# Decode attention with a gated MLP on one core: the output products move between the halves of the next head's score products, and an output weight moves from the fourth row to the fifth

## The chip, the core and the metric

The kernel runs on one core of a Trainium2 chip. The metric is device time in microseconds of one execution, the median of several runs. A core has five engines with instruction streams of their own: TensorE (PE; PEld is its loading of weights), VectorE (DVE), ScalarE (ACT), GpSimd (POOL) and SyncE (SP), which here only issues transfers. They wait for one another through semaphores. Sixteen DMA engines carry the transfers from HBM into SBUF, the on-chip memory of 128 partitions.

## The reference

One token attends to a cache of 8192 positions in 32 heads of 192, and a gated MLP follows:

```python
def _A_ref(x, k_cache, v_cache, wq, wo):          # x: layer norm of the token, 640 wide
    q = (x @ wq).reshape(B, Sq, H, Dh)            # H = 32, Dh = 192
    scores = einsum("bhqd,bhkd->bhqk", q, k_cache) * (Dh ** -0.5)   # Sk = 8192
    p = softmax(scores)
    o = einsum("bhqk,bhkd->bhqd", p, v_cache)
    return o.reshape(B, Sq, H * Dh) @ wo
h = x + _A_ref(layernorm(x), ...)
h2 = h + _B_ref(layernorm(h), W_gate, W_up, W_down)   # (gate * (gate > 0) * up) @ W_down, F = 1536
```

All data are float32. Nearly all bytes are the keys and values: 6.3 MB each for every head.

## The kernel before

The host packs keys, values and weights into long rows, so that each transfer is one block of 128 partitions with up to 16320 columns of 4 bytes, 8160 KB. SBUF has room for three such rows, the slots X, Y and Z. Thirty heads go in ten turns of three units; a prologue row (`row_p`, in Y) has the first head's query weights and keys, and a tail has the last head and the MLP.

The heads of a turn are called a, b, c. In a unit TensorE makes the scores of its head (`pe_k`, two halves of 12 products into `sc`) and the product of the values with the exponentials of the head before it (`pe_v`, 32 products into `po`). The rows of a turn:

- row 1, into X: keys of a, query weights of b, values 0 to 7 of the head before a
- row 2, into Z: that head's values 8 to 31, its output weights (`woa`), first half of b's keys
- row 3, into Y: second half of b's keys, query weights of c, values 0 to 23 of a
- row 4, into X: values 24 to 31 of a, its output weights (`wob`), keys of c
- row 5, into Y: query weights of the next a, all values of b, its output weights (`woc`)

A unit on TensorE, `pe_unit` (L220) and `pe_unit2` (L343) for the third, runs: scores, both halves; values 0 to 23; the next query (`pe_q`, `pe_t`), which waits for VectorE; values 24 to 31; then a wait for ScalarE's copy `ob` of the value products, the output products `pe_o` (into `od`, six small products), a wait for the exponentials, and `pe_l`, their sum (into `pl`). Only then do the next unit's scores begin.

VectorE (`dve_unit`, L404) follows: it transposes both score halves (L400), finds the maximum `mp` (L408), multiplies the next query weights by the token (`dve_d1`, five instructions, L392 and L394), takes the maximum `m` (L411), which the exponentials need, copies `od` to `oc`, adds the output weights times `oc` to `accs` (two instructions, L414 and L415), and makes the factor `mrl` from the sum (L416, L417).

SP (`turn`, L554) issues the five rows in order on one queue. Ahead of each issue it waits until the slot was released and the row before in that slot has landed: row 3 for `free[5]`, row 4 for `free[1]`, row 5 for `free[2]` and `free[3]`, the next rows 1 and 2 together for `free[4]`. VectorE gives `free[4]` behind its second transpose in the third unit (`relay`), `free[2]` at the same place in the second, and `free[5]` at the end of the turn; TensorE gives `free[1]` and `free[3]`, in two steps each, with certain value products and ahead of `pe_q`.

Of the kernel before, what the change touches and what calls it, by code (L numbers as in the profile page):

```python
# [27 lines left out]
W_4 = 8 * PW + OW + KW  # L28
W_5 = QW + KW + OW
# [8 lines left out]
def pack(inputs):  # L38
# [26 lines left out]
    for i in range(NTURN):  # L65
        a, b, c = 3 * i + 1, 3 * i + 2, 3 * i + 3
        va, vb, vv = vc[a - 1], vc[b - 1], vc[c - 1]
        rows[0][i] = cat(kw[a], qw(b), va[:, :8 * PW])
        rows[1][i] = cat(va[:, 8 * PW:], ow(a - 1), kw[b][:, :12 * 512])
        rows[2][i] = cat(kw[b][:, 12 * 512:], qw(c), vb[:, :24 * PW])  # L70
        rows[3][i] = cat(vb[:, 24 * PW:], ow(b - 1), kw[c])
        rows[4][i] = cat(qw(c + 1), vv, ow(c - 1))
# [13 lines left out]
def build(nc, arrays):  # L86
# [46 lines left out]
    def wait(eng, s, n, sub=0, **kw):  # L133
        w = eng.wait_ge(s, n)  # L134
        if sub:
            w.then_inc(s, -sub)
        return w
# [8 lines left out]
    slots = {"p": Y, 1: X, 2: Z, 3: Y, 4: X, 5: Y}  # L146
    k_at = lambda t, off: (lambda half, i: t[:, off + (i + 12 * half) * 512:off + (i + 12 * half + 1) * 512])
    pr_at = lambda t, off, i: t[:, off + i * PW:off + (i + 1) * PW]
# [13 lines left out]
    wob = cut(X, 8 * PW, OW)  # L162
    kc = lambda half, i: cut(X, 8 * PW + OW + (12 * half + i) * 512, 512)
    wqa = cut(Y, 0, QW)
    vcc = lambda i: cut(Y, QW + i * PW, PW)
    woc = cut(Y, QW + KW, OW)
# [14 lines left out]
    def pe_k(blk, before=(None, None)):  # L181
        for half in range(2):
            if before[half] is not None:
                wait(te, before[half], 16)
            for part in range(3):
                for g in range(4):
                    m = te.matmul(sc[Q(g), half * 512:half * 512 + 512], qs[:, 32 * part:32 * part + 32],  # L187
                                  blk(half, part * 4 + g), start=(part == 0), stop=(part == 2))
            op(m, inc=p2d)
# [27 lines left out]
    def pe_l():  # L217
        op(te.matmul(pl[:, 0:1], ones, vec["rs"], start=True, stop=True), inc=p2d)

    def pe_unit(kblk, kwait, vblk, vwait, freed, q_next=True, split=24, inc_at=None):  # L220
        pe_k(kblk, kwait)
        pe_v(vblk, 0, 8, inc_at=inc_at)
        if vwait[0] is not None:
            wait(te, vwait[0], 16)
        pe_v(vblk, 8, 24, inc_at=inc_at)
        if q_next:
            wait(te, d2p, 2, 2)
            if freed is not None:
# [5 lines left out]
        if vwait[1] is not None:  # L234
            wait(te, vwait[1], 16)
        pe_v(vblk, 24, 32, last=p2a)
        n = 2 if q_next else 1
        wait(te, a2p, n, n)
        pe_o()
        wait(te, a2p, 1, 1)  # L240
        pe_l()

    def pe_warm(n):
        for _ in range(n):
            for g in range(4):
                te.matmul(pl[Q(g), :], ones[:, 0:32], ident.rearrange("p c -> p c")[:, None, :].to_broadcast([P, 4, P]),
                          start=True, stop=True)

    def tensor_program():
        wait(te, cst_pe, 1, 1)  # L250
        wait(te, land[0], 16)
# [7 lines left out]
        pe_k(kp)  # L259
# [3 lines left out]
        wait(te, a2p, 2, 2)  # L263
        pe_l()
        with te.Fori(0, NTURN):
            wait(te, land[1], 16)
            pe_unit(ka, (None, None), va, (land[2], None), free[1], inc_at=(7, free[1]))
            pe_unit(kb, (None, land[3]), vb, (None, land[4]), free[3], inc_at=(23, free[3]))
            pe_unit2()
        wait(te, tl["t1"], 16, 16)  # L270
        pe_k(kt)
        pe_v(vt, 0, 8, inc_at=(7, fin))
        wait(te, tl["t2a"], 16, 16)
        pe_v(vt, 8, 24)
        wait(te, d2p, 1, 1)
        pe_t()
        pe_v(vt, 24, 32, last=p2a)
# [65 lines left out]
    def pe_unit2():  # L343
        pe_k(kc)
        wait(te, land[5], 16)
        pe_v(vcc, 0, 24)
        wait(te, d2p, 2, 2)
        pe_q()
        pe_t()
        pe_v(vcc, 24, 32, last=p2a)  # L350
        wait(te, a2p, 2, 2)
        pe_o()
        wait(te, a2p, 1, 1)
        pe_l()

# [25 lines left out]
    def settle(extra=0):  # L381
# [15 lines left out]
    def dve_scores():  # L397
        for half in range(2):
            s = slice(half * 512, half * 512 + 512)
            dv(ve.transpose(st[:, s], sc[:, s]), w=pd())  # L400

    scores = st.rearrange("p (r u) -> p r u", u=16)[:, :, 0]

    def dve_unit(wo_t, w_next, relay=None, q_wait=None):  # L404
        dve_scores()
        if relay is not None:
            wait(ve, ds, cnt.n).then_inc(relay, 1)
        dv(ve.reduce_max(vec["mp"], scores, axis=AX.X), w="self", inc=d2p)  # L408
        if w_next is not None:
            dve_d1(w_next, first=q_wait)  # L410
        dv(ve.reduce_max(vec["m1"], pt[:, 0:P], axis=AX.X, negate=True), w=pd(), inc=d2a)  # L411
        if wo_t is not None:
            dv(ve.tensor_copy(oc, od[:, 0:2]), w=pd())  # L413
            dv(STT(accs[:, 0:D], wo_t[:, 0:D], oc[:, 0:1], accs[:, 0:D], op0=ALU.mult, op1=ALU.add), w="self")  # L414
            dv(STT(accs[:, D:OW], wo_t[:, D:OW], oc[:, 1:2], accs[:, D:OW], op0=ALU.mult, op1=ALU.add))  # L415
        dv(ve.reciprocal(vec["rl"], pl[:, 0:1]), w=pd())  # L416
        dv(ve.tensor_scalar(mrl, id32[:, 0:2], vec["rl"], None, op0=ALU.mult), w="self")  # L417

# [8 lines left out]
    def vector_program():  # L427
        dv(ve.memset(po[:, 0:PW], 0.0))
        dv(ve.memset(accs, 0.0))
        dv(ve.reduce_sum(id32, ident.rearrange("p (g c) -> p c g", c=32), axis=AX.X), w=(cst_ve, 1))  # L430
        wait(ve, cst_ve, 1, 1)
        wait(ve, land[0], 16)
# [10 lines left out]
        dve_scores()  # L443
        dv(ve.reduce_max(vec["mp"], scores, axis=AX.X), w="self", inc=d2p)
        dve_d1(wq1)
        dv(ve.reduce_max(vec["m1"], pt[:, 0:P], axis=AX.X, negate=True), w=pd(), inc=d2a)
        ve.sem_inc(free[5], 1)
        dv(ve.reciprocal(vec["rl"], pl[:, 0:1]), w=pd())
        dv(ve.tensor_scalar(mrl, id32[:, 0:2], vec["rl"], None, op0=ALU.mult), w="self")
        settle()  # L450
        with ve.Fori(0, NTURN):
            dve_unit(woa, wqb)
            dve_unit(wob, wqc, relay=free[2])
            wait_row5 = (land[5], 16)
            dve_unit(woc, wqa, relay=free[4], q_wait=wait_row5)
            settle()
            ve.sem_inc(free[5], 1)
        dve_scores()
        dv(ve.reduce_max(vec["mp"], scores, axis=AX.X), w="self", inc=d2p)
        dv(ve.reduce_max(vec["m1"], pt[:, 0:P], axis=AX.X, negate=True), w=pd(), inc=d2a)  # L460
        dv(ve.tensor_copy(oc, od[:, 0:2]), w=pd())
        dv(STT(accs[:, 0:D], wot[:, 0:D], oc[:, 0:1], accs[:, 0:D], op0=ALU.mult, op1=ALU.add), w="self", inc=d2p)
        dv(STT(accs[:, D:OW], wot[:, D:OW], oc[:, 1:2], accs[:, D:OW], op0=ALU.mult, op1=ALU.add), inc=d2p)
        dv(ve.reciprocal(vec["rl"], pl[:, 0:1]), w=pd())
        dv(ve.tensor_scalar(mrl, id32[:, 0:2], vec["rl"], None, op0=ALU.mult), w="self")
# [34 lines left out]
    def scalar_program():  # L500
# [3 lines left out]
        act_qs()  # L504
        act_exp()
# [40 lines left out]
    def sync_program():  # L546
        load(Y[:, 0:W_P], dram["row_p"], land[0])
# [3 lines left out]
        wait(sp, free[5], 1, 1)  # L551
        wait(sp, land[0], 16, 16)

        def turn(i):  # L554
            load(Y[:, 0:W_3], r3[i], land[3])
            wait(sp, free[1], 2, 2)
            wait(sp, land[1], 16, 16)
            load(X[:, 0:W_4], r4[i], land[4])
            wait(sp, free[2], 1, 1)
            wait(sp, land[2], 16, 16)  # L560
            wait(sp, free[3], 2, 2)
            wait(sp, land[3], 16, 16)
            load(Y[:, 0:W_5], r5[i], land[5])
            wait(sp, free[4], 1, 1)
            wait(sp, land[4], 16, 16)

        with sp.Fori(0, NTURN - 1) as i:
            turn(i)
            load(X[:, 0:W_1], r1[i + 1], land[1])
            load(Z[:, 0:W_2], r2[i + 1], land[2])  # L570
            wait(sp, free[5], 1, 1)
            wait(sp, land[5], 16, 16)
# [35 lines left out]
```

## Time and profile before

| | |
|---|---|
| median of 3 runs | 1045.81 us (1042.98 to 1047.77) |
| the profiled execution, its own time | 1047.05 us |
| its span, first to last instruction | 1045.8 us |
| TensorE busy | 562.2 us, 54% |
| VectorE busy | 189.7 us, 18% |
| ScalarE busy | 40.8 us, 4% |
| mean granted TensorE clock | 0.742 |
| moved by DMA | 446.07 MB, mean 427 GB/s |

The span covers the profiled execution only, and times inside it count from its first instruction. In rows of the timeline the first number is the start, the second the length, both in us; behind the operands stands how many instructions are merged, and in brackets how long the engine was idle before and what ended it. A matmul of float32 shows up as two records, so a unit's 24 score products are x48. In rows of windows stand the bounds, the length, the busy time of PE, PEld, DVE, ACT and POOL, the granted TensorE clock as a share of full speed, the DMA engines' share and GB/s.

### The profile page before, as it was taken

To read this page: it belongs to the slowest core of one execution; us is meant where nothing else is said; L and a number is where in the kernel's file an instruction comes from. 1 tells how busy PE (TensorE), PEld (TensorE's weight loads), DVE (VectorE), ACT (ScalarE), POOL (GpSimd) and SP (SyncE) were. 2 spreads that over 40 slices of the span, in tenths; PEclk is the share of its full clock that TensorE was granted. 3 is DMA by queue.
4 is the path that set the end of the run, shared out by engine and by line. 5 is a ranking of instruction groups with operands and counts; after the bars stand their busy time and mean duration, and the time that the engine had idled before them with its cause. 6 is when DMAs were issued, how large, how long until landed. Compare 5 with 4: busy or idle time off the path is not lost. (4 is left out here: it accounts for less than half of the span.)

```text
span 1045.8 us, 10227 instructions
## 1 busy us (share of the span) xinstructions
PE 562.2 (54%) x4480; PEld 181.9 (17%) x4480; DVE 189.7 (18%) x474; ACT 40.8 (4%) x136; POOL 1.2 (0%) x11
## 2 busy tenths in 40 slices
PE   0645646555373464565644736645465456464566
PEld 0212112111121111121111201211121121121123
DVE  1311212111122122121121211211122112121111
ACT  1000000000000000000000000000000000000000
POOL 0000000000000000000000000000000000000000
PEclk9886767667777677686687776677867767676788
DMA  9999999999999999999999999999999999999998
GB/s 399 438 438 424 419 439 439 436 412 429 434 408 432 439 440 432 437 429 416 439 432 432 413 437 414 433 434 439 424 413 439 437 421 436 422 437 431 414 424 344
DMA packets 8800, 446.07 MB, mean 427 GB/s; under 512 B 980, under 2 KB 1112, under 8 KB 1240
## 3 DMA queue, kind: packets, MB, share of 16 engines
q1 hardware_dynamic: 8788, 445.94, 99.1%
q8 instruction: 7, 0.11, 0.0%
q14 instruction: 1, 0.01, 0.0%
q10 hardware_dynamic: 4, 0.00, 0.0%
HBM read 445.94 MB, written 0.00 MB: 426 GB/s over the span
## 5 line engine op out<-in xcount | busy, mean ns | idle before, releaser
L187 PE MATMUL sc<-slot_x,qs 128*32 128x512 f32 x1008 | 152.3, 767 | 95.1 <-DMA slot_x<-row 85.0
L194 PE MATMUL po<-slot_y,p 128*2 128x384 f32 x1152 | 122.3, 579 | 46.5 <-DMA slot_y<-row 43.7
L194 PE MATMUL po<-slot_z,p 128*2 128x384 f32 x560 | 69.9, 650 | 107.9 <-DMA slot_z<-row 103.3
L400 DVE STREAM_TRANSPOSE st<-sc 128x512 f32<-128x512 f32 x64 | 45.9, 717 | 338.3 <-PE sc L187 338.3
L187 PE MATMUL sc<-slot_y,qs 128*32 128x512 f32 x288 | 55.7, 937 | 75.6 <-DMA slot_y<-row 75.1
L194 PE MATMUL po<-slot_x,p 128*2 128x384 f32 x336 | 43.5, 652 | 94.6 <-DMA slot_x<-row 94.6
L187 PEld LDWEIGHTS sc<-slot_x,qs 128*32 128x32 f32 x1008 | 36.0, 136 | 193.3 <-issue 107.4
L194 PEld LDWEIGHTS po<-slot_y,p 128*2 128x2 f32 x1152 | 30.5, 96 | 138.0 <-issue 84.0
L411 DVE TENSOR_REDUCE m<-pt 128x1 f32<-128x128 f32 x30 | 8.8, 292 | 209.6 <-PE pt L206 209.6
L194 PEld LDWEIGHTS po<-slot_z,p 128*2 128x2 f32 x560 | 14.7, 100 | 153.1 <-DMA slot_z<-row 110.5
L413 DVE COPY oc<-od 128x2 f32<-128x2 f32 x30 | 4.8, 160 | 197.8 <-PE od L213 197.8
L486 ACT COPY qs<-q_ps 128x96 f32<-128x96 f32 x32 | 7.7, 239 | 765.3 <-ACTq L134 765.3
L394 DVE SCALAR_TENSOR_TENSOR prod<-slot_y,xn,prod 128x192 f32<-128x192 f32 x88 | 36.9, 419 | 3.1
L210 PE MATMUL od<-mrl,ob 128*128 128x1 f32 x128 | 22.1, 277 | 24.7 <-PEq L134 24.7
L187 PEld LDWEIGHTS sc<-slot_y,qs 128*32 128x32 f32 x288 | 11.6, 157 | 114.9 <-DMA slot_y<-row 84.2
L210 PEld LDWEIGHTS od<-mrl,ob 128*128 128x128 f32 x128 | 20.3, 227 | 53.1 <-issue 53.1
L194 PEld LDWEIGHTS po<-slot_x,p 128*2 128x2 f32 x336 | 8.3, 94 | 118.4 <-DMA slot_x<-row 96.5
L187 PE MATMUL sc<-slot_z,qs 128*32 128x512 f32 x240 | 27.8, 596 | 0.0
L490 ACT COPY ob<-po 128x384 f32<-128x384 f32 x32 | 15.3, 479 | 192.1 <-ACTq L134 192.1
L201 PE MATMUL q_ps<-pat,prod 128*128 128x96 f32 x64 | 15.5, 326 | 8.5 <-PEq L134 8.5
L394 DVE SCALAR_TENSOR_TENSOR prod<-slot_x,xn,prod 128x192 f32<-128x192 f32 x40 | 16.8, 419 | 1.4
L201 PEld LDWEIGHTS q_ps<-pat,prod 128*128 128x128 f32 x64 | 10.1, 199 | 31.0 <-issue 31.0
(106 smaller groups left out, 249.6 us busy)
## 6 DMA issues: line engine op xcount, KB each, us to landing
slot_x<-row SPq DMA_DIRECT2D x20, 8160.0 KB, 36.8
slot_z<-row SPq DMA_DIRECT2D x10, 8160.0 KB, 42.5
slot_y<-row SPq DMA_DIRECT2D x10, 8160.0 KB, 45.5
slot_y<-row SPq DMA_DIRECT2D x10, 7104.0 KB, 26.9
slot_x<-row_t SPq DMA_DIRECT2D x1, 7680.0 KB, 22.8
slot_y<-row_p SPq DMA_DIRECT2D x1, 7136.0 KB, 19.6
slot_z<-row_t2a SPq DMA_DIRECT2D x1, 5088.0 KB, 34.5
slot_y<-row_up SPq DMA_DIRECT2D x1, 3840.0 KB, 44.4
```

The lines of the kernel that those rows point to most:

```text
L187: m = te.matmul(sc[Q(g), half * 512:half * 512 + 512], qs[:, 32 * part:32 * part + 32], blk(half, part * 4 + g), start=(part == 0), stop=( ...
L194: m = te.matmul(po[32 * g:32 * g + 2, 0:PW], p[:, 2 * i:2 * i + 2], blk(i), start=(i < 4), stop=(i >= 28))
L201: te.matmul(q_ps[:, 0:96], prod[:, 0:P], pat[:, 0, :], start=True, stop=False)
L210: te.matmul(od[:, 0:1], ob[:, k * DH:k * DH + P], mrl[:, k:k + 1], start=(k == 0), stop=(k == 1))
L394: dv(STT(prod, w3[:, j, :], xn[:, j:j + 1], prod, op0=ALU.mult, op1=ALU.add), w="self", inc=d2p if j == DJ - 1 else None)
L400: dv(ve.transpose(st[:, s], sc[:, s]), w=pd())
L411: dv(ve.reduce_max(vec["m1"], pt[:, 0:P], axis=AX.X, negate=True), w=pd(), inc=d2a)
L413: dv(ve.tensor_copy(oc, od[:, 0:2]), w=pd())
L486: op(ac.copy(qs, q_ps[:, 0:96]), inc=a2p)
L490: op(ac.copy(ob, po[:, 0:PW]), inc=a2p)
```

## The change

Three things are changed together.

TensorE: `pe_o` and `pe_l` of a unit move into the next unit, between the two halves of its scores. The scores' first half waits only for the query. `pe_unit2` goes, the third unit uses `pe_unit`, and the waits for rows are given as a table of places.

VectorE: `dve_unit` now begins with the copy `oc` and the factor `mrl` of the head before, then come the transposes, `mp`, the next query, the output weights and `m`. `free[4]` is given once the second score half is done, ahead of the second transpose; `free[2]` and `free[5]` are given behind the output weights, `free[5]` hence in the first unit of the next turn.

Rows: `wob` moves from row 4 (now 15360 columns) to row 5 (now 15168). SP waits for `free[2]` ahead of the next row 1 and no longer ahead of row 5. The prologue's row counts on row 5's semaphore, and the first unit adds a product with zeros (`mrl` is set to zero, `ob` is copied from zeros).

```diff
-W_4 = 8 * PW + OW + KW
-W_5 = QW + KW + OW
+W_4 = 8 * PW + KW
+W_5 = 2 * OW + QW + KW
...
+    def pe_unit(kblk, vblk, rows, freed=None, freed_at=None, q_next=True):
+        def landed(n):
+            if n in rows:
+                s, sub = rows[n]
+                wait(te, s, 16, sub)
+
+        wait(te, a2p, 1, 1)
+        landed("k0")
+        pe_k(kblk, 0)
+        wait(te, a2p, 1, 1)
+        pe_o()
+        wait(te, a2p, 1, 1)
+        pe_l()
+        landed("k1")
+        pe_k(kblk, 1)
+        landed("v0")
...
+    def dve_unit(w_out, w_next=None, freed_k=None, freed_wo=None, row=None):
+        k0 = pd()
+        dve_out()
+        dve_mrl()
+        dve_t(0, w=k0)
+        k1 = pd()
+        if freed_k is not None:
+            wait(ve, *k1).then_inc(freed_k, 1)
+            dve_t(1)
+        else:
+            dve_t(1, w=k1)
+        dve_mp()
+        if row is not None:
+            wait(ve, row, 16)
+        if w_next is not None:
+            dve_d1(w_next)
+        dve_wo(w_out)
+        if freed_wo is not None:
+            wait(ve, ds, cnt.n).then_inc(freed_wo, 1)
+        dve_m1()
...
         with ve.Fori(0, NTURN):
-            dve_unit(woa, wqb)
-            dve_unit(wob, wqc, relay=free[2])
-            wait_row5 = (land[5], 16)
-            dve_unit(woc, wqa, relay=free[4], q_wait=wait_row5)
+            dve_unit(woc, wqb, freed_wo=free[5])
+            dve_unit(woa, wqc, freed_wo=free[2])
+            dve_unit(wob, wqa, freed_k=free[4], row=land[5])
             settle()
-            ve.sem_inc(free[5], 1)
...
         def turn(i):
+            wait(sp, free[5], 1, 1)
+            wait(sp, land[5], 16, 16)
             load(Y[:, 0:W_3], r3[i], land[3])
             wait(sp, free[1], 2, 2)
             wait(sp, land[1], 16, 16)
             load(X[:, 0:W_4], r4[i], land[4])
-            wait(sp, free[2], 1, 1)
-            wait(sp, land[2], 16, 16)
             wait(sp, free[3], 2, 2)
             wait(sp, land[3], 16, 16)
             load(Y[:, 0:W_5], r5[i], land[5])
+            wait(sp, free[2], 1, 1)
+            wait(sp, land[2], 16, 16)
             wait(sp, free[4], 1, 1)
             wait(sp, land[4], 16, 16)
```

The order on TensorE from the end of the second unit into the third, before (`po` are value products, `od` output products, `pl` the sum, `sc` scores; the new kernel's line numbers differ):

```order
L194 MATMUL po<-slot_x,p 2x384 x8
L210 MATMUL od<-mrl,ob 128x1 x2
L213 MATMUL od<-mrl,ob 64x1 x4
L218 MATMUL pl<-rs,ones 128x1
L187 MATMUL sc<-slot_x,qs 32x512 x24
L194 MATMUL po<-slot_y,p 2x384 x24
```

and now, at the same place:

```order
L187 MATMUL po<-slot_x,p 2x384 x8
L180 MATMUL sc<-slot_x,qs 32x512 x12
L203 MATMUL od<-mrl,ob 128x1 x2
L206 MATMUL od<-mrl,ob 64x1 x4
L211 MATMUL pl<-rs,ones 128x1
L180 MATMUL sc<-slot_x,qs 32x512 x12
L187 MATMUL po<-slot_y,p 2x384 x24
```

The output products and the sum have moved behind the first twelve score products.

VectorE in the first unit of a turn, before (`accs` rows are those with the output weights):

```order
L400 STREAM_TRANSPOSE st<-sc 128x512 x2
L408 TENSOR_REDUCE mp<-st 128x1
L392 TENSOR_SCALAR prod<-slot_x,xn 128x192
L394 SCALAR_TENSOR_TENSOR prod<-slot_x,xn,prod 128x192 x4
L411 TENSOR_REDUCE m<-pt 128x1
L413 COPY oc<-od 128x2
L414 SCALAR_TENSOR_TENSOR accs<-slot_z,oc,accs 128x640
L415 SCALAR_TENSOR_TENSOR accs<-slot_z,oc,accs 128x320
L416 RECIPROCAL rl<-pl 128x1
L417 TENSOR_SCALAR mrl<-id,rl 128x2
```

and now:

```order
L373 COPY oc<-od 128x2
L380 RECIPROCAL rl<-pl 128x1
L381 TENSOR_SCALAR mrl<-id,rl 128x2
L385 STREAM_TRANSPOSE st<-sc 128x512 x2
L388 TENSOR_REDUCE mp<-st 128x1
L365 TENSOR_SCALAR prod<-slot_x,xn 128x192
L367 SCALAR_TENSOR_TENSOR prod<-slot_x,xn,prod 128x192 x4
L376 SCALAR_TENSOR_TENSOR accs<-slot_y,oc,accs 128x640
L377 SCALAR_TENSOR_TENSOR accs<-slot_y,oc,accs 128x320
L391 TENSOR_REDUCE m<-pt 128x1
```

The output weights read here are those of row 5 of the turn before (slot Y); with them Y is released, for row 3.

SP in the loop, before (ISA rows are waits alone):

```order
L544 DMA slot_y<-row 128x16320
L544 DMA slot_x<-row 128x16320 [waits free1,land1]
L544 ISA [waits free2,land2,free3,land3]
L544 DMA slot_y<-row 128x14208
L544 ISA [waits free4,land4]
L544 DMA slot_x<-row 128x16320
L544 DMA slot_z<-row 128x16320
L567 REGISTER_ALU [waits free5,land5]
```

and now:

```order
L533 ISA [waits free5,land5]
L533 DMA slot_y<-row 128x16320
L533 ISA [waits free1,land1]
L533 DMA slot_x<-row 128x15360
L533 ISA [waits free3,land3]
L533 DMA slot_y<-row 128x15168
L533 ISA [waits free2,land2,free4,land4]
L533 DMA slot_x<-row 128x16320
L533 DMA slot_z<-row 128x16320
```

The wait for `free[2]` has moved past row 5's issue; the widths of rows 4 and 5 are new.

More of the change, by code (lines that the diff above doesn't have):

```diff
@@ L179, in build, with pe_k @@
     te = nc.tensor
[L181 to L189, printed above, removed]
+    def pe_k(blk, half):
+        for part in range(3):
+            for g in range(4):
+                m = te.matmul(sc[Q(g), half * 512:half * 512 + 512], qs[:, 32 * part:32 * part + 32],
+                              blk(half, part * 4 + g), start=(part == 0), stop=(part == 2))
+        op(m, inc=p2d)
     def pe_v(blk, i0, i1, last=None, inc_at=None):
@@ L218, in pe_l @@
         op(te.matmul(pl[:, 0:1], ones, vec["rs"], start=True, stop=True), inc=p2d)
[L220 to L225, printed above, removed]
+    def pe_unit(kblk, vblk, rows, freed=None, freed_at=None, q_next=True):
[13 more added lines that the diff above has]
+        landed("v0")
+        at = None if freed is None else (freed_at, freed)
+        pe_v(vblk, 0, 8, inc_at=at)
+        landed("v8")
+        pe_v(vblk, 8, 24, inc_at=at)
         if q_next:
             wait(te, d2p, 2, 2)
-            if freed is not None:
+            if freed is not None and freed_at < 24 and freed is not fin:
                 te.sem_inc(freed, 1)
@@ L233, in pe_unit @@
         pe_t()
-        if vwait[1] is not None:
-            wait(te, vwait[1], 16)
+        landed("v24")
         pe_v(vblk, 24, 32, last=p2a)
[L237 to L247, printed above, removed]
     def tensor_program():
         wait(te, cst_pe, 1, 1)
-        wait(te, land[0], 16)
         wait(te, pre, 1, 1)
@@ L258, in tensor_program @@
         wait(te, a2p, 1, 1)
-        pe_k(kp)
+        wait(te, land[5], 16)
+        pe_k(kp, 0)
+        pe_k(kp, 1)
         wait(te, d2p, 2, 2)
@@ L262, in tensor_program @@
         pe_t()
-        wait(te, a2p, 2, 2)
-        pe_l()
         with te.Fori(0, NTURN):
[L266 to L277, printed above, removed]
+            pe_unit(ka, va, {"k0": (land[1], 0), "v8": (land[2], 0)}, free[1], 7)
+            pe_unit(kb, vb, {"k1": (land[3], 0), "v24": (land[4], 0)}, free[3], 23)
+            pe_unit(kc, vcc, {"v0": (land[5], 0)})
+        pe_unit(kt, vt, {"k0": (tl["t1"], 16), "v8": (tl["t2a"], 16)}, fin, 7, q_next=False)
         wait(te, a2p, 1, 1)
@@ L395, in dve_d1, with dve_out @@
                inc=d2p if j == DJ - 1 else None)
[L397 to L400, printed above, removed]
     scores = st.rearrange("p (r u) -> p r u", u=16)[:, :, 0]
[L404 to L415, printed above, removed]
+    def dve_out():
+        dv(ve.tensor_copy(oc, od[:, 0:2]), w=pd())
@@ L416, in dve_unit, with dve_wo, dve_mrl, dve_t @@
+    def dve_wo(w, inc=None):
+        dv(STT(accs[:, 0:D], w[:, 0:D], oc[:, 0:1], accs[:, 0:D], op0=ALU.mult, op1=ALU.add), w="self", inc=inc)
+        dv(STT(accs[:, D:OW], w[:, D:OW], oc[:, 1:2], accs[:, D:OW], op0=ALU.mult, op1=ALU.add), inc=inc)
+    def dve_mrl():
         dv(ve.reciprocal(vec["rl"], pl[:, 0:1]), w=pd())
         dv(ve.tensor_scalar(mrl, id32[:, 0:2], vec["rl"], None, op0=ALU.mult), w="self")
+    def dve_t(half, w=None):
+        s = slice(half * 512, half * 512 + 512)
+        return dv(ve.transpose(st[:, s], sc[:, s]), w=w)
@@ L429, in vector_program @@
         dv(ve.memset(accs, 0.0))
+        dv(ve.memset(mrl, 0.0))
         dv(ve.reduce_sum(id32, ident.rearrange("p (g c) -> p c g", c=32), axis=AX.X), w=(cst_ve, 1))
         wait(ve, cst_ve, 1, 1)
-        wait(ve, land[0], 16)
+        wait(ve, land[5], 16)
         dv(ve.reduce_sum(vec["s1"], xT, axis=AX.X), w="self", inc=pre)
@@ L504, in scalar_program @@
         act_qs()
+        op(ac.copy(ob, po[:, 0:PW]), inc=a2p)
         act_exp()
```

62 lines of the change are left out of this document (20 added, 42 removed).

## The prediction

> **What bounds the kernel now.** I read the page first, for the transfers as a whole; then the timeline, for the moment at which each row of weights lands and the moment at which the next is issued; then the windows between landings. Two rows of the page say how full the queue is:
>
> ```profile
> span 1045.8 us, 10227 instructions
> q1 hardware_dynamic: 8788, 445.94, 99.1%
> ```
>
> The transfers take 99.1% of sixteen engines' span, so nothing that only TensorE, VectorE or ScalarE do is worth anything by itself. What can still be won is time in which the queue is not full. To find it I take as landing of a row the start of the first instruction that waited for it, and give the time from one landing to the next as a window (the first number is its bounds, the second its length, the last but one the share of the DMA engines; packets are counted where they start, so only the length is used). One whole turn, beginning with row 1:
>
> ```profile
> 209.40:230.02 20.62, 9.34 (x86) 3.61 (x86) 4.08 (x11) 1.11 (x4) 0.00 (x0) 0.68 0.95 408
> 230.02:249.26 19.24, 8.53 (x64) 2.08 (x65) 3.60 (x8) 0.00 (x0) 0.00 (x0) 0.68 1.00 434
> 249.26:268.54 19.28, 11.56 (x94) 3.75 (x94) 2.82 (x7) 1.11 (x4) 0.00 (x0) 0.77 1.00 433
> 268.54:287.82 19.28, 9.01 (x79) 2.67 (x79) 3.18 (x8) 0.24 (x1) 0.00 (x0) 0.77 0.98 426
> 287.82:304.92 17.10, 12.72 (x79) 4.21 (x79) 3.53 (x9) 0.87 (x3) 0.00 (x0) 0.68 1.03 429
> ```
>
> Rows 1 to 4 have the same 8160 KB. Rows 2, 3 and 4 take 19.24 to 19.28 us, row 1 takes 20.62: 1.35 us more than 19.27. Row 5 has 14208 of 16320 columns, 16.78 us by that rate; here it takes 17.10. So a full queue lands a full row every 19.27 us, and the time over it is lost at row 1. The other windows from row 5's landing to row 1's, the last of them to the first row of the tail:
>
> ```profile
> 304.92:326.54 21.62, 9.33 (x85) 3.61 (x85) 4.08 (x11) 1.11 (x4) 0.00 (x0) 0.67 1.00 432
> 401.17:420.44 19.27, 9.28 (x85) 3.39 (x86) 4.08 (x11) 1.11 (x4) 0.00 (x0) 0.68 1.00 434
> 495.05:515.43 20.38, 10.12 (x85) 3.50 (x85) 4.08 (x11) 1.11 (x4) 0.00 (x0) 0.67 1.04 452
> 590.06:609.33 19.27, 10.40 (x85) 3.58 (x86) 4.08 (x11) 1.11 (x4) 0.00 (x0) 0.68 1.00 434
> 683.92:703.51 19.59, 9.33 (x85) 3.54 (x85) 4.08 (x11) 1.11 (x4) 0.00 (x0) 0.69 0.98 427
> 778.22:798.62 20.40, 10.19 (x86) 3.57 (x86) 4.08 (x11) 1.11 (x4) 0.00 (x0) 0.67 0.95 410
> 873.23:893.63 20.40, 10.47 (x86) 3.58 (x86) 4.08 (x11) 1.11 (x4) 0.00 (x0) 0.67 0.98 422
> 968.31:988.22 19.91, 9.02 (x86) 3.39 (x87) 4.08 (x11) 1.11 (x4) 0.00 (x0) 0.76 0.97 416
> ```
>
> Over 19.27 us (over 18.14 for the tail's row, which has 15360 columns) they lose 1.35, 2.35, 0, 1.11, 0, 0.32, 1.13, 1.13 and 1.77 us, together **9.16 us**. Why row 1 and no other? The timeline has its issues:
>
> ```profile
> 207.09 0.33 SPq L544 DMA_DIRECT2D slot_x<-row  x1
> 302.49 0.33 SPq L544 DMA_DIRECT2D slot_x<-row  x1
> 395.55 0.33 SPq L544 DMA_DIRECT2D slot_x<-row  x1
> 491.58 0.33 SPq L544 DMA_DIRECT2D slot_x<-row  x1
> 221.97 0.33 SPq L544 DMA_DIRECT2D slot_y<-row  x1
> 250.95 0.33 SPq L544 DMA_DIRECT2D slot_x<-row  x1
> 183.26 0.33 SPq L544 DMA_DIRECT2D slot_y<-row  x1
> ```
>
> Row 1 goes out at 207.09, 2.31 us before row 5, the last thing ahead of it, has landed at 209.40: I call that its **lead**. The next leads are 2.43, 5.62 and 3.47 us, with losses of 2.35, 0 and 1.11. Row 3 (221.97) leads row 2's landing at 249.26 by 27.29 us, row 4 (250.95) row 3's at 268.54 by 17.59, row 5 (183.26, a turn earlier) row 4's at 192.60 by 9.34; rows 3 and 4 lose nothing, row 5 0.3 us once. A lead of 2.3 to 3.5 us is too little in most turns, and 5.6 was enough.
>
> **The change, part by part.** First what row 1 waits for, SP's wait on the third unit's release. These rows run from the landing of row 4 to the issue:
>
> ```profile
> 192.60 2.74 PE L194 MATMUL po<-slot_x,p 128*2 128x384 f32 x16 [8.74 <-DMA slot_x<-row]
> 195.49 0.48 ACT L490 COPY ob<-po 128x384 f32<-128x384 f32 x1 [11.52 <-ACTq L134]
> 196.11 0.98 PE L210 MATMUL od<-mrl,ob 128*128 128x1 f32 x4 [0.77 <-PEq L134]
> 197.55 0.58 PE L218 MATMUL pl<-rs,ones 128*128 128x1 f32 x2
> 198.06 7.85 PE L187 MATMUL sc<-slot_x,qs 128*32 128x512 f32 x48
> 206.00 0.72 DVE L400 STREAM_TRANSPOSE st<-sc 128x512 f32<-128x512 f32 x1 [1.86 <-PE sc L187]
> ```
>
> The value products end at 195.34, the output products and the sum stand from 196.11 to 198.13, the scores from 198.06 to 205.91, the second transpose ends at 206.72 and the row is issued 0.37 us later: 14.49 us from landing to issue. Four things change.
>
> (1) Row 4 loses 960 of 16320 columns and lands 960/16320 x 19.27 = 1.13 us sooner; row 5 gains them and lands when it did, the bytes of a turn being the same. Added transfer time: nothing.
>
> (2) The first score half no longer waits for the copy of the output and the exponentials: the 2.72 us from 195.34 to 198.06 go. The output products and the sum then cost their own length between the halves. At 0.50 clock that is 2.02 us (196.11 to 198.13); at full clock the same pair of rows is shorter:
>
> ```profile
> 218.28 0.58 PE L210 MATMUL od<-mrl,ob 128*128 128x1 f32 x4 [0.77 <-PEq L134]
> 219.13 0.38 PE L218 MATMUL pl<-rs,ones 128*128 128x1 f32 x2
> ```
>
> From 218.28 to 219.51 it is 1.23 us. What they wait for (ScalarE's copy, done 0.63 us after the value products, and the exponentials right behind it) lies beside the first half, which is 2.6 us even at its fastest (block under 4). Net 0.7 to 1.5 us sooner.
>
> (3) VectorE gives the row free when the scores end, ahead of the second transpose, not behind it: 205.91 plus 0.4 us for the wait and the issue, in place of 207.09, 0.8 us sooner.
>
> So landing to issue is 2.74 + 7.85 + 1.23 to 2.02 + 0.4 = 12.2 to 13.0 us, and row 5 lands 15168/16320 x 19.27 = 17.91 us after row 4. **Row 1's lead becomes 4.9 to 5.7 us** where it was 2.31. It may be more: with no gap ahead of the scores TensorE should come to its full clock earlier, and the scores at full clock throughout would take 5.2 us, a lead of 7.6 to 8.3.
>
> (4) Row 3 pays. Its slot is now also read by the third output row, whose products with the output weights move into the next turn's first unit, behind the transposes and the next query. So row 3's issue moves from the end of a turn to the middle of the next turn's first unit. Its path begins when row 1 lands:
>
> ```profile
> 230.02 7.24 PE L187 MATMUL sc<-slot_x,qs 128*32 128x512 f32 x48 [10.51 <-DMA slot_x<-row]
> 234.76 0.72 DVE L400 STREAM_TRANSPOSE st<-sc 128x512 f32<-128x512 f32 x1 [13.62 <-PE sc L187]
> 237.34 0.72 DVE L400 STREAM_TRANSPOSE st<-sc 128x512 f32<-128x512 f32 x1 [1.86 <-PE sc L187]
> 238.61 1.78 DVE L394 SCALAR_TENSOR_TENSOR prod<-slot_x,xn,prod 128x192 f32<-128x192 f32 x4
> 219.45 0.88 DVE L414 SCALAR_TENSOR_TENSOR accs<-slot_y,oc,accs 128x640 f32<-128x640 f32 x1
> 220.25 0.54 DVE L415 SCALAR_TENSOR_TENSOR accs<-slot_y,oc,accs 128x320 f32<-128x320 f32 x1
> ```
>
> From 230.02 to the end of the query's products at 240.39 are 10.37 us; the inserted output products and sum add 1.23 to 2.02, the two weight rows 1.34 (219.45 to 220.79), the wait and issue 0.4: 13.3 to 14.1 us. Row 2 lands 19.24 us after row 1, so **row 3's lead falls from 27.29 to 5.1 to 5.9 us**. Queued behind it on SP are row 4 and row 5; row 4's own release comes only after row 2's landing (250.95 against 249.26), so it is not held. The wait for Z's release is moved on SP from ahead of row 5 to ahead of row 1; it comes in the second unit, ahead of the third unit's release that row 1 waits for anyway, and row 5, which no longer waits for it, had its 9.34 us in hand. VectorE's maximum now stands behind the two weight rows (1.34 us), but it waits for TensorE's transpose, which in every unit follows at least 16 value products. All of this lies beside transfers: zero, as long as both leads hold.
>
> A lead of 5 us isn't in the trace: the nearest are 3.47 (1.11 lost) and 5.62 (0 lost). For row 3 the loss at 5.1 to 5.9 us is thus between 0 and some 1.1 a turn; I take 0, since 5.62 is nearer. For row 1 the same bounds hold, and I take 0 too.
>
> **Sum.** 9.16 us go, nothing comes. The profiled execution took 1047.05 us, 1.25 more than its span; 1047.05 - 9.16 = **1037.9 us**. It stood 1.24 us above the median of 1045.81; as the losses at row 1 are what differs from turn to turn, I count that difference as more of them, and the time without them as the same.
>
> The first turn is special, since TensorE gets to row 1 only after the first head's scores:
>
> ```profile
> 43.00 6.89 PE L187 MATMUL sc<-slot_x,qs 128*32 128x512 f32 x48
> 60.17 4.24 PE L194 MATMUL po<-slot_z,p 128*2 128x384 f32 x32 [9.00 <-DMA slot_z<-row]
> ```
>
> From 43.00 the same 13.3 to 14.1 us give an issue of row 3 at 56.3 to 57.1, and sooner by up to the 2.72 us of part (2), since a sum and its wait no longer stand ahead of these scores; row 2 lands at 60.17. The lead is 3.1 to 6.6 us, and at most one turn's loss (0 to 1.1 us, by the leads of 5.62 and 3.47) hangs on it, which I leave at 0.
>
> **A rule against it.** Row 1 follows an issue 2.31 us ahead and still loses 1.35 us. In the Trainium skill, "DMA: Bandwidth & Descriptors", section "Latency and other measured facts", the first byte of a transfer issued from SP is put at about 600 ns after its issue. By that rule every lead here is ample, the losses have another cause, and the change gives nothing. The rows speak against it: of the five rows of the turn shown, the four with leads over 9 us land on time but for 0.3 us once.
>
> **The rivals.** *Nothing gained* (the losses aren't from late issue): 1047.05 less nothing, 1044 to 1047 with the spread of runs. For it: a lead of 3.47 us lost nearly as much as one of 2.31, so the lead alone doesn't set the size. Against: rows 2 to 4 of these turns never lose. 9%.
>
> *Part gained*: leads near 5 us still lose up to half of what they do now, at row 1 or row 3: 1047.05 - 4.6 = 1042.5, from 1040.5 to 1044. 15%.
>
> *Slower, the loss moves to row 3*: TensorE waits 10.51 us for row 1 and begins its scores at 0.50 clock. The second half takes 2.58 us at full clock (234.76 to 237.34), so a half at half clock 5.2. If output products and sum, small as they are, keep the clock down, the scores are 10.4 in place of 7.24 and the pair 2.02: landing to issue becomes 14.1 + 3.2 = 17.3, the lead 1.9 us, and row 3 loses what row 1 loses at 2.3 to 2.4: 1.35 and 2.35 in the rows above. With 1.35 a turn for row 3 in ten turns, 13.5 us come for 9.2 that go: 1051.4. It decides from a lead of about 3.5 us down. These two windows bear on it, the first with the small products, the second with scores alone:
>
> ```profile
> 196.33:199.74 3.41, 3.41 (x22) 2.08 (x26) 1.81 (x5) 0.03 (x1) 0.00 (x0) 0.50 1.00 433
> 199.74:203.15 3.41, 3.41 (x20) 0.79 (x16) 0.00 (x0) 0.00 (x0) 0.00 (x0) 0.50 0.85 367
> ```
>
> The second one was enough to bring the clock up (the scores that began at 198.06 took 7.85, not 10.4); the first, though busy throughout, was not. So the insertion can delay the clock. But the first half alone takes up to 5.2 us at half clock, longer than one such window, and will mostly have raised it before the insertion comes. The Trainium skill, "TensorE: Matmul & The Clock Gate", section "What's actually happening", has a free-running window of 3413 ns of activity that releases the clock; the trace agrees with the 3.41 us steps, and by it only starts that straddle a window badly would be held down. 8%.
>
> **How the numbers follow.** Forecast 68%: 1036.4 (the 0.3 of row 5 and a little at the start gone too) to 1040.5. With part gained up to 1043 the range is 1036 to 1043. About 0.5%, or 5.2 us, is what a measurement of this kernel can tell from no change: faster means under 1040.6. Faster: 68% and a third of part gained, 73%; within: the rest of that and nothing gained, 19%; slower 8%.
>
> **What would show it.** Right: windows from row 5's landing to row 1's of 19.27 us in every turn, row 1 issued 5 to 8 us before row 5 lands, row 3 issued 4 to 6 us before row 2 lands, and the window of row 3 still 19.27. Wrong: windows of row 1 still over 20 us at leads of 5 us (the cause isn't the lead), or windows of row 3 over 20 us with scores of 10 us in the first unit (the loss has moved).

## The result and the profile after

The changed kernel takes 1038.85 us in the median of 6 runs (1037.96 to 1039.9), the kernel before 1046.47 (6 runs beside them, 1042.98 to 1048.82). The ratio is 0.9928, 95% interval 0.991 to 0.9947: 0.7% faster, 7.6 us. Medians here and below are over all executions, while the ratios leave out one of a variant that took 1061.36 us at a granted clock of 0.529. The profiled execution took 1039.63 us, 7.42 less than that of before. The same two rows of the page, of the new kernel:

```profile
span 1038.3 us, 10306 instructions
q1 hardware_dynamic: 8788, 445.94, 99.4%
```

The windows from row 5's landing to row 1's in the first, second, third and last turn of the loop, and to the tail's first row, which has 15360 columns:

```profile
115.68:134.95 19.27, 7.85 (x72) 2.21 (x72) 3.53 (x8) 1.11 (x4) 0.00 (x0) 0.77 1.00 434
209.56:228.84 19.28, 8.69 (x71) 2.36 (x71) 3.52 (x8) 1.11 (x4) 0.00 (x0) 0.68 1.00 433
303.45:322.73 19.28, 7.83 (x71) 2.21 (x71) 3.53 (x8) 1.11 (x4) 0.00 (x0) 0.77 1.00 433
866.81:886.09 19.28, 7.75 (x71) 2.21 (x71) 3.53 (x8) 1.11 (x4) 0.00 (x0) 0.77 1.00 433
960.71:978.94 18.23, 8.59 (x71) 2.34 (x72) 3.53 (x8) 1.11 (x4) 0.00 (x0) 0.69 0.98 424
```

Every one has the length of a full queue to within 0.1 us (19.27, for the tail's row 18.14); before, they lost up to 2.35 us. Row 3, whose lead shrank, in the first three turns:

```profile
60.05:79.61 19.56, 10.83 (x94) 3.86 (x94) 1.47 (x5) 1.11 (x4) 0.00 (x0) 0.76 1.01 435
154.22:173.51 19.29, 11.48 (x94) 3.92 (x94) 1.47 (x5) 1.11 (x4) 0.00 (x0) 0.77 1.01 439
248.12:267.39 19.27, 10.66 (x93) 3.79 (x94) 1.46 (x5) 1.11 (x4) 0.00 (x0) 0.77 1.02 440
```

It loses 0.29 us in the first turn and nothing after. The path from row 4's landing to row 1's issue, in the turn whose rows of before were shown:

```profile
191.65 2.74 PE L187 MATMUL po<-slot_x,p 128*2 128x384 f32 x16 [8.99 <-DMA slot_x<-row]
194.17 4.23 PE L180 MATMUL sc<-slot_x,qs 128*32 128x512 f32 x24
198.33 0.61 PE L203 MATMUL od<-mrl,ob 128*128 128x1 f32 x4
199.20 0.38 PE L211 MATMUL pl<-rs,ones 128*128 128x1 f32 x2
199.51 2.78 PE L180 MATMUL sc<-slot_x,qs 128*32 128x512 f32 x24
202.71 0.33 SPq L533 DMA_DIRECT2D slot_x<-row  x1
```

The scores follow the value products without a gap, the pair between the halves takes 1.25 us (198.33 to 199.58), and the second half runs at full clock (2.78 us; the granted clock is 1.00 from 197.14 to 207.38). From landing to issue it is 11.06 us instead of 14.49, and the lead over row 5's landing at 209.56 is 6.85 us instead of 2.31. Row 3's path from row 1's landing in the next unit:

```profile
228.84 5.35 PE L180 MATMUL sc<-slot_x,qs 128*32 128x512 f32 x24 [10.59 <-DMA slot_x<-row]
234.12 0.86 PE L203 MATMUL od<-mrl,ob 128*128 128x1 f32 x4
235.56 2.78 PE L180 MATMUL sc<-slot_x,qs 128*32 128x512 f32 x24
242.18 0.55 DVE L377 SCALAR_TENSOR_TENSOR accs<-slot_y,oc,accs 128x320 f32<-128x320 f32 x1
243.11 0.33 SPq L533 DMA_DIRECT2D slot_y<-row  x1
```

14.27 us to the issue, a lead of 5.01 us over row 2's landing at 248.12.

**Where the sum went.** From row 2's first landing to the tail's first row it was 60.17 to 988.22 before, 928.05 us, and is now 60.05 to 978.94, 918.89: 9.16 us less. From there to the output's issue these windows (before, then after) took longer:

```profile
988.22:1044.37 56.15, 40.78 (x423) 15.59 (x423) 7.86 (x23) 3.81 (x9) 0.00 (x0) 0.82 0.94 401
```

```profile
978.94:1036.88 57.94, 43.26 (x437) 17.29 (x437) 9.56 (x28) 3.81 (x9) 0.00 (x0) 0.80 0.92 393
```

1.79 us came back in the tail. At its end, in the timeline before and after:

```profile
1034.22 3.43 PE L320 MATMUL sc<-slot_x,hc 128*32 128x384 f32 x40 [1.26 <-PEq L134]
```

```profile
1026.02 5.13 PE L306 MATMUL sc<-slot_x,hc 128*32 128x384 f32 x40 [2.42 <-PEq L134]
1035.93 0.48 PE L325 MATMUL q_ps<-slot_x,guT 128*32 128x160 f32 x8
```

The gate products began 46.00 us after the tail's first row before and 47.08 now, and took 5.13 us instead of 3.43, so the last products came later. 1.08 of the 1.79 us are thus the landing of the gate's row. The trace records a completion of each row by each of the sixteen DMA engines: of this row's, fifteen came by 1024.81 and the last only at 1025.88. A packet of 16 KB on the queue that carries instructions (the page's "instruction" queue) took 1.02 us of one engine at 1020.41; that it was the late engine isn't recorded. The rest goes with the granted clock, 1.00 before and 0.64 now as the gate products run:

```profile
1034.20:1037.60 3.40, 3.38 (x40) 1.43 (x40) 0.00 (x0) 0.00 (x0) 0.00 (x0) 1.00 0.94 399
1025.65:1029.06 3.41, 3.04 (x24) 1.42 (x28) 0.00 (x0) 0.00 (x0) 0.00 (x0) 0.64 0.96 408
```

From the last completion of the tail's first row to the output's issue it was 56.3, 56.3 and 57.8 us in the three traces with the old tail, and 56.6 to 58.6 in ten with the new one, the variants below among them. The two overlap, with means 1.0 us apart: part is spread, and whether the change, which also alters the order in the tail, costs something there is open.

### The profile page after: what moved, and what is told of

Read it like the earlier page. It is cut to its first block, busy times and chain, and to the rows that moved or that the text cites. A ratio compares the mean times of both kernels' runs of the same rounds, so it can differ in the third digit from the quotient of the medians.

```text
span 1038.3 us, 10306 instructions
## 1 busy us (share of the span) xinstructions
PE 547.4 (53%) x4492; PEld 176.3 (17%) x4492; DVE 188.2 (18%) x478; ACT 41.2 (4%) x137; POOL 1.2 (0%) x11
## 5 line engine op out<-in xcount | busy, mean ns | idle before, releaser
L187 PE MATMUL po<-slot_y,p 128*2 128x384 f32 x1152 | 117.9, 562 | 80.2 <-DMA slot_y<-row 77.4
L187 PE MATMUL po<-slot_z,p 128*2 128x384 f32 x560 | 72.5, 671 | 91.7 <-DMA slot_z<-row 88.4
L203 PEld LDWEIGHTS od<-mrl,ob 128*128 128x128 f32 x132 | 18.1, 199 | 34.2 <-issue 34.2
L365 DVE TENSOR_SCALAR prod<-slot_y,xn 128x192 f32<-128x192 f32 x22 | 6.9, 315 | 65.4 <-DMA slot_y<-row 65.3
L376 DVE SCALAR_TENSOR_TENSOR accs<-slot_y,oc,accs 128x640 f32<-128x640 f32 x21 | 18.5, 879 | 0.0
```

The costliest lines, as they stand in the source:

```text
L187: m = te.matmul(po[32 * g:32 * g + 2, 0:PW], p[:, 2 * i:2 * i + 2], blk(i), start=(i < 4), stop=(i >= 28))
L203: te.matmul(od[:, 0:1], ob[:, k * DH:k * DH + P], mrl[:, k:k + 1], start=(k == 0), stop=(k == 1))
L365: dv(ve.tensor_scalar(prod, w3[:, 0, :], xn[:, 0:1], None, op0=ALU.mult), w=first)
L376: dv(STT(accs[:, 0:D], w[:, 0:D], oc[:, 0:1], accs[:, 0:D], op0=ALU.mult, op1=ALU.add), w="self", inc=inc)
```

## The experiments

The theory: a row loses time when it is issued too short a time ahead of the landing of the row before it, whichever part of the change lengthens that lead. The rivals: the first byte comes so soon after the issue that a lead of 1 us would do; the losses come from something else in the old order; only row 1 is sensitive.

**Delaying row 1 alone.** VectorE fills an unused tile n times between the end of the third unit's scores and the release. n is 6, 10, 14 and 20:

```diff
-            wait(ve, *k1).then_inc(freed_k, 1)
+            wait(ve, *k1)
+            for _ in range(n):
+                dv(ve.memset(gu, 0.0), w="self")
+            wait(ve, ds, cnt.n).then_inc(freed_k, 1)
             dve_t(1)
```

> The new kernel with six small fills by VectorE (128x384, about 0.4 us each, working from the 0.38 us of the fill of po in the trace of before) between the end of the third unit's scores and the release for row 1; nothing else differs, and the output is the same. Row 1's lead over the landing of row 5, 6.8 and 7.7 us in alternate turns of the new kernel, becomes about 4.4 and 5.3. Lead theory (row 1 lost time because it was issued too late): no loss or under 0.5 us a turn, the time within 3 us of the new kernel's 1039. Rival, first byte soon after the issue (only a lead under 1 us loses): no loss, the same time. Rival, the loss was not from the lead: no loss, the same time.

> Ten fills: lead about 2.8 and 3.7 us, where the kernel before had 2.3 to 3.5. Lead theory: the loss of before comes back, 0.5 to 1.5 us a turn, windows of row 1 of 19.8 to 20.8 us, the time about 1045 to 1050. First byte soon: no loss, 1039. Not from the lead: no loss, 1039.

> Fourteen fills: lead about 1.2 and 2.1 us. Lead theory: 1.5 to 2.5 us lost a turn, the time 1054 to 1064. First byte soon: under 0.5 us a turn, 1039 to 1044. Not from the lead: no loss, 1039.

> Twenty fills: row 1 is issued about 0.3 to 1.2 us after row 5 has landed. Lead theory: loss per turn = the lateness plus a constant of 2 to 3 us, so 2.5 to 4 us a turn, the time 1064 to 1079. First byte soon: lateness plus under 1.5 us, so 1 to 2.5 us a turn, 1049 to 1064. Not from the lead: under 1.2 us a turn, the lateness alone.

Measured, with leads and losses of turns 2 to 10 as in the prediction:

| fills | row 1's leads, us | lost at row 1 in nine turns, us | time, us |
|---|---|---|---|
| 0 (the changed kernel) | 6.9 to 7.8 | 0.1 | 1039.63 |
| 6 | 3.5 to 5.1 | 1.4 | 1041.22 |
| 10 | 1.4 to 3.0 | 13.5 | 1054.24 |
| 14 | -0.5 to 0.9 | 18.1 | 1060.34 |
| 20 | -2.6 to -2.4 | 46.3 | 1090.46 |

Each is one profiled execution. A fill took 0.51 us, not 0.4, so all leads are shorter than expected, and the times with ten and twenty fills lie above what I had expected at the longer leads. Two windows of row 1 with ten fills, where the issues were 2.42 and 2.96 us ahead of row 5:

```profile
211.73:232.78 21.05, 7.80 (x71) 2.21 (x72) 3.52 (x8) 1.11 (x4) 0.00 (x0) 0.74 0.97 419
591.69:612.92 21.23, 8.96 (x71) 2.42 (x72) 3.52 (x8) 1.11 (x4) 0.00 (x0) 0.66 1.03 440
```

```profile
209.31 0.33 SPq L536 DMA_DIRECT2D slot_x<-row  x1
588.73 0.33 SPq L536 DMA_DIRECT2D slot_x<-row  x1
```

1.78 and 1.96 us are lost at leads of 2.4 to 3.0; the two other rows at such leads in this trace lost 0.45 and 2.12. Before the change it was 0 to 2.4 in the loop. With twenty fills the row is late outright:

```profile
214.44:238.78 24.34, 9.20 (x72) 2.42 (x72) 5.98 (x15) 1.11 (x4) 0.00 (x0) 0.64 0.92 386
```

```profile
216.96 0.33 SPq L536 DMA_DIRECT2D slot_x<-row  x1
```

It was issued 2.52 us after row 5 had landed and lost 5.07: the lateness and 2.55 more. The fills hold VectorE up as well, but in these four kernels row 3 kept leads of 4.9 us and more in turns 2 to 10 and lost nothing there; row 1, and the tail's first row, which waits for the same release, lost the time. So the lead brings the loss back, and the rivals of another cause and of a lead of 1 us being enough fall.

That doesn't speak against a quick first byte. In the Trainium skill, "DMA: Bandwidth & Descriptors", section "Latency and other measured facts", the first byte is put at about 600 ns after an issue from SP. The trace is near it: row 1's first packet starts 0.96 us after its issue began at 216.96, 0.63 after the issue's end. Here 4 us from 216.90 are cut into 40 slices; a packet counts in the slice in which it starts, 653 for one packet:

```profile
GB/s 0 0 0 0 0 0 0 0 0 0 4570 3264 653 653 0 653 0 653 0 0 0 0 0 0 0 0 0 0 0 0 0 0 0 0 0 0 0 0 0 0
DMA packets 16, 1.04 MB, mean 261 GB/s; under 512 B 0, under 2 KB 0, under 8 KB 0
```

The first sixteen packets start between 217.92 and 218.68 and take 2.5 to 3.6 us, where the next ones take 2.41. The last of them ends 4.54 us after the issue began, 2.1 more than a packet of a full queue takes, which is most of the 2.55. What fails is the inference, weighed in the prediction as a rule against it, that any lead beyond the first byte is ample: here a queue that had run dry wasn't at its full rate with its first packets.

**Delaying row 3 alone.** The same fills, 5 and 9, ahead of `free[5]`:

```diff
         dve_wo(w_out)
+        if freed_wo is free[5]:
+            for _ in range(n):
+                dv(ve.memset(gu, 0.0), w="self")
         if freed_wo is not None:
```

> The new kernel with five fills of about 0.4 us ahead of the release for row 3, behind the output weights of the first unit; the output is the same. Row 3's lead over row 2's landing, 5.0 and 5.8 us in alternate turns, becomes about 3.0 and 3.8. Lead theory, the same bounds for every row: 0.5 to 1.2 us lost a turn in row 3's window, the time about 1044 to 1050. Rival, only row 1 is sensitive (it is issued together with row 2): no loss, 1039.

> Nine fills ahead of the release for row 3: lead about 1.4 and 2.2 us, about the 1.9 of my slower rival. Lead theory: 1.4 to 2.4 us lost a turn in row 3's window, the time 1052 to 1062, slower than the kernel before. Rival, only row 1 is sensitive: no loss, 1039.

The first took 1669.43 us and says nothing of the lead. Its page:

```profile
span 1668.1 us, 10361 instructions
L180 PE MATMUL sc<-slot_x,qs 128*32 128x512 f32 x1008 | 463.7, 2077 | 6.5 <-DMA slot_x<-row 6.5
```

A score product took 2077 ns where the changed kernel's mean is 743, and TensorE was busy 97% of the span. Its trace has no record of the granted clock; the clock of 1.00 in the next text stands only for this absence. Run again:

> The same kernel as row3_late_5, whose one execution had TensorE at a quarter of its speed throughout (score halves of 10 us at a recorded clock of 1.00) and so says nothing of the lead. Expected as there: row 3's lead about 3.0 and 3.8 us, 0.5 to 1.2 us lost a turn, 1044 to 1050; if row 3 is not sensitive, 1039. If the slow TensorE belongs to this kernel, it comes again.

It took 1047.06 us, with leads of row 3 of 2.6 to 3.7 us and 7.0 us lost at row 3 in turns 2 to 10 (0 to 2.2 a turn). Nine fills took 1056.97 us, with leads of 0.7 to 1.5 us and 13.9 us lost at row 3; a window of it and its issue, 1.49 us ahead of the landing at 157.49:

```profile
157.49:178.23 20.74, 11.10 (x93) 3.85 (x94) 1.46 (x5) 1.11 (x4) 0.00 (x0) 0.75 0.95 409
```

```profile
156.00 0.33 SPq L536 DMA_DIRECT2D slot_y<-row  x1
```

Row 3 is as sensitive as row 1. This is what my slower rival said of a short lead at row 3: about 10 us slower than the kernel before at a lead of 1 us.

**One part at a time.** The early release alone, in the kernel before:

```diff
+            k = pd()
+            if half == 1 and early is not None:
+                wait(ve, *k).then_inc(early, 1)
+                dv(ve.transpose(st[:, s], sc[:, s]))
+            else:
+                dv(ve.transpose(st[:, s], sc[:, s]), w=k)
...
-            dve_unit(woc, wqa, relay=free[4], q_wait=wait_row5)
+            dve_unit(woc, wqa, early=free[4], q_wait=wait_row5)
```

> The kernel before with one part of the change alone: the release for row 1 ahead of the second transpose of the third unit. Lead theory: row 1's lead grows by 0.8 us, from 2.3 to 3.5 to 3.1 to 4.3, and the loss falls from about 1.0 to between 0.3 and 0.7 us a turn: 2 to 6 us faster than before, some 1041 to 1044. If the loss isn't from the lead: the time of before, 1043 to 1048. Orders alone: I expect no change of any other row's window.

> The kernel before with the early release alone, timed. Its one profile lost 6.6 us at row 1, against 7.4 in the profile of before, with leads of 2.6 to 6.6 us. Lead theory: 0.5 to 4 us faster than before, a ratio of 0.996 to 0.9995, since half of the turns keep a lead under 3 us. If it is not worth anything: a ratio of 1.000 within its interval.

One execution took 1045.87 us; the median of 12 was 1044.72, ratio 0.9983, interval 0.9965 to 1.000: a gain that can't be told from none. The first trace shows why its turns differ. Two of its third units:

```profile
480.74 8.28 PE L187 MATMUL sc<-slot_x,qs 128*32 128x512 f32 x48
489.43 0.33 SPq L549 DMA_DIRECT2D slot_x<-row  x1
492.06 4.05 PE L194 MATMUL po<-slot_y,p 128*2 128x384 f32 x48 [3.05 <-DMA slot_y<-row]
...
576.64 5.36 PE L187 MATMUL sc<-slot_x,qs 128*32 128x512 f32 x48
582.41 0.33 SPq L549 DMA_DIRECT2D slot_x<-row  x1
588.77 1.46 PE L194 MATMUL po<-slot_y,p 128*2 128x384 f32 x8 [6.78 <-DMA slot_y<-row]
```

In the one the scores began at half clock, took 8.28 us and left a lead of 2.63; in the other the clock was up, they took 5.36 and left 6.36. The first of these turns lost 2.8 us, the second nothing. Of the other leads of 2.6 us one lost 2.5 and one nothing; those of 6.4 and more lost nothing.

The products put back ahead of the scores, with the new rows and the new release:

```diff
-        landed("k0")
-        pe_k(kblk, 0)
         wait(te, a2p, 1, 1)
         pe_o()
         wait(te, a2p, 1, 1)
         pe_l()
+        landed("k0")
+        pe_k(kblk, 0)
         landed("k1")
...
```

> The new kernel with the output products and the sum put back ahead of the first score half; rows and release stay new. The scores of the third unit then wait again for the copy and the exponentials. Row 1's lead by the terms of the sum: 17.92 us from row 4's landing to row 5's, less 2.74, 2.72, 7.85 and 0.4, is 4.2 us, a little less or more with the clock. Lead theory, with the losses seen at leads of 3.7 to 4.4 when the release was delayed (0.0 to 0.6 us a turn): 1039 to 1045, so the narrower fourth row and the release alone give at least half of the gain. If taking the products out of the way is what counts: the time of before, 1044 to 1049.

1042.01 us in the median of 10 runs, ratio 0.9954, interval 0.9935 to 0.9973. In its profile (1042.79 us) row 1's leads were 4.2 to 8.9 us and lost 0.4 us in nine turns, the first turn lost 1.2 at row 3 (lead 4.0) and 1.4 at row 5 (lead 8.9, so not for want of lead). So rows and release alone bring 0.46% of the 0.72% gained, by the interval 0.27 to 0.65; at one lead, 4.24 us, 0.23 us was lost.

The release put back behind the second transpose, all else new:

```diff
-            wait(ve, *k1).then_inc(freed_k, 1)
-            dve_t(1)
+            dve_t(1, w=k1)
+            wait(ve, ds, cnt.n).then_inc(freed_k, 1)
```

> The new kernel with the release for row 1 put back behind the second transpose. Row 1's lead falls by 0.8 us, from 6.8 and 7.7 to about 6.0 and 6.9. Lead theory: no loss, 1037 to 1040; the early release is not needed. If the release ahead of the transpose is what counts: losses at row 1 of 0.5 us or more a turn, 1044 or above.

1039.13 us, leads of 6.2 to 7.1, nothing lost at row 1: not needed beside the other two.

The rows of before, with the output weights added ahead of the transposes:

```diff
...
         dve_out()
+        dve_wo(w_out)
+        if freed_wo is not None:
+            wait(ve, ds, cnt.n).then_inc(freed_wo, 1)
         dve_mrl()
...
         if freed_k is not None:
+            wait(ve, ds, cnt.n)
             wait(ve, *k1).then_inc(freed_k, 1)
...
             dve_d1(w_next)
-        dve_wo(w_out)
-        if freed_wo is not None:
-            wait(ve, ds, cnt.n).then_inc(freed_wo, 1)
         dve_m1()
```

> The new kernel with the rows of before (the second output weight in row 4, 16320 columns, row 5 with 14208) and the output weights added right behind the copy of the output products, ahead of the transposes, so that row 4's slot still comes free with the scores. Row 1's lead loses 1.13 us by the wider row 4, to about 5.7 and 6.6; row 3's lead grows by about 3 to 5 us, since its release no longer stands behind the transposes and the query. Lead theory: no loss at rows 1 and 3, the time of the new kernel, 1037 to 1041. If the narrower fourth row was what counted: losses of row 1 of up to 1 us a turn, 1042 to 1049.

1038.22 us in one execution, nothing lost at either row. Row 1's leads were 5.9 to 6.8 us and row 3's 11.2 to 12.1; the issues of one turn, ahead of landings at 209.25 and 247.80:

```profile
203.38 0.33 SPq L534 DMA_DIRECT2D slot_x<-row  x1
235.74 0.33 SPq L534 DMA_DIRECT2D slot_y<-row  x1
```

The wider fourth row does no harm in this order. This order keeps both leads over 5.8 us in every turn, where the changed kernel's row 3 has 5.0; its time can't be told from the changed kernel's.

**All leads together.** Rows 1 and 3 (and the tail's first row) of these kernels, first turns and the execution of 1669 us left out:

| lead, us | rows | mean loss, us | largest |
|---|---|---|---|
| under -2 | 10 | 5.1 | 5.4 |
| -1 to 0 | 2 | 3.3 | 3.4 |
| 0 to 1 | 12 | 1.8 | 2.3 |
| 1 to 2 | 10 | 1.3 | 1.9 |
| 2 to 3 | 14 | 1.5 | 2.8 |
| 3 to 4 | 18 | 0.8 | 2.2 |
| 4 to 4.8 | 11 | 0.3 | 1.7 |
| 4.8 to 6 | 61 | 0.0 | 0.1 |
| over 6 | 109 | 0.0 | 0.04 |

Part of the scatter below 4.8 us can be read from the traces. The first of the sixteen engines is done with a row 0.3 to 3.9 us ahead of the last (median 1.8), whose completion is the landing, and it has nothing to move until the next row is issued. Counted to the first completion in place of the landing, lead and loss go together closely: with 0 to 0.5 us the next row's first completion is 1.4 to 1.9 us late (20 rows), with 1 to 1.5 us 0.5 to 1.3 (9 rows), from 3 us up at most 0.2 (162 rows). The 4.8 us are thus about 3 us ahead of the first engine's end and the 1.8 between the first and the last. How much of it reaches the landing isn't settled: two rows of the early release, with leads of 2.59 and 2.62 us, lost 0.01 and 2.82 while the completions ahead of them stood 2.6 and 0.7 us apart.

Not every loss comes from a lead. In the first turn row 2, issued 38 us ahead, landed 0.8 to 1.2 us late in every one of these traces, each time with a 16 KB packet of the instruction queue, about 1 us long, at 48.2 to 48.6 us.

## Why the prediction was right

*What bounds the kernel*: right. The losses sat at row 1, and they are gone: 9.16 us by the sum, 9.16 us less between the first landing of row 2 and the tail.

*Row 1's lead*: 4.9 to 5.7 us was forecast, up to 8.3 if the clock came up sooner; measured 6.9 to 7.8. Parts (1) and (3) hold as priced. In part (2) the pair cost 1.25 us, the lower end, and the clock did come up sooner, so that part gave more than its 0.7 to 1.5 us. The variants show that no single part was needed in full: without (3) nothing is lost, without (1) nothing (there with the weights added earlier), without (2) little in turns 2 to 10.

*Row 3's lead*: 5.1 to 5.9 us was forecast, 5.0 to 6.0 measured. I chose a loss of 0 between the ends of 0 and 1.1, by the nearer row of 5.62. That was right and closer than it looked: losses begin below some 4.8 us, so that 0.2 us less would have begun to cost.

*The first turn*: forecast 0, 0.29 lost, within its bounds.

*The sum*: 9.16 us were forecast off the execution, 7.42 came off. The step that failed is "nothing comes": the loop gave its 9.16 (the first turn's 0.29 is made up for by row 5, which no longer loses its 0.3 and 0.1), and the tail took 1.79 more, 1.08 of it at the gate's row. A tail that varies by 2.3 us was no term of mine. The prediction of 1037.9 was 1.73 us under the profiled execution and 0.95 under the median; that the loop gave just the 9.16 of the sum is partly chance, since it counted neither the 0.29 that came nor row 5's 0.3 and 0.1 that went.

*The rule against it* was outweighed rightly: at leads of 2 to 3 us 11 of 14 rows lose time. But the rule on the first byte isn't at fault; the trace is near it. What doesn't follow is that a lead beyond it costs nothing.

*The slower rival* was right about what a short lead of row 3 costs, and about where it begins (12 of 18 rows at leads of 3 to 4 us lose time, on average 0.8; 1.3 us a row at 1 to 2 us). Whether the inserted products can hold the clock down is shown by no run, as the condition did not arise, and by little: in the unit shown the first half ran at half clock to its end at 234.19, and the granted clock rose at 234.69, within the inserted pair. The second half then took 2.78 us, at full clock. That half at half clock is also why row 3's path came to 14.27 us, past my 14.1. The Trainium skill's window of 3413 ns ("TensorE: Matmul & The Clock Gate", section "What's actually happening") and the trace agree there: the first half began at half clock and was 5.35 us long.

Not settled is why equal leads below 4.8 us lose between 0 and 2.8 us at the landing; the first of the sixteen completions explains a part.

## What to carry to other kernels

A queue that a profile calls 99% busy can still lose a per cent: measure each transfer from landing to landing against the longest run without loss, and look at how long before the end of the transfer ahead each one was issued. Here a lead of 5 us was always enough from the second turn on, and 3 us mostly not, so a release is worth moving until the lead is past that point and not further. When a wait is shortened in one place, work out the lead of the transfer that pays for it just as carefully: a delay of 4 to 5 us at row 3's release turned this gain into a loss of about 10 us.

## What the runs showed of the hardware

A row issued 2.5 us after the queue had run dry cost its lateness and about 2.5 us. Its first packet started 0.96 us after the issue began, but the sixteen first packets took up to 3.6 us in place of 2.41.

The sixteen DMA engines end one row up to 3.9 us apart. In the changed kernel that distance was 0.8 us at the first row of the loop and 1.8 to 1.9 from the second on, in every turn.

Leads come in two values in alternate turns (6.9 and 7.8 us for row 1, 5.0 and 5.8 for row 3). The granted clock changes at steps of 3.41 us; a turn without loss is 93.9 us, 27.5 such steps, so that alternate turns meet the steps half a step apart. That is worked out, not tried.

One execution of a kernel that otherwise took 1047 us had its score products at about a quarter of their speed from end to end (halves of about 10 us, 2.58 at full clock), with no clock recorded. In the Trainium skill, "TensorE: Matmul & The Clock Gate", section "Seeing it yourself", records of the clock are called unreliable on trn2 and a clock stuck at a quarter for over 50 us is told of; here the products were slow for all of the 1668 us, and that the clock was the cause isn't shown.
